# Attention, one-expert MoE and GLU on one core: scores made transposed in narrow array tiles, and fewer weight conversions in the last batch

## The chip, the cores and the metric

One core of one Trainium2 chip runs the whole kernel as one program. The metric is device time in microseconds (us), median over runs. The engines are named as the profile names them: PE (TensorE matmul), PEld (its weight loads), DVE (VectorE), ACT (ScalarE), POOL (GpSimd) and SP (SyncE, which issues nearly all DMAs here).

## The reference, cut to what matters

```python
B, H, S, Dh, M = 8, 8, 576, 64, 32
a   = softmax(phi, axis=2)                      # over the 576 positions
k_m = einsum('bhsm,bhsd->bhmd', a, k)           # 32 pooled keys of each head
v_m = einsum('bhsm,bhsd->bhmd', a, v)
attn = softmax(q @ k_m^T / 8, axis=-1)          # the scores: 576 x 32 of each head
x   = attn @ v_m                                # 4608 x 512
x   = moe(x)        # top-1 expert of 8, hidden 1024, relu, times its gate weight
out = (sigmoid(x @ w_gate) * (x @ w_val)) @ w_out    # GLU, width 1536
```

## The kernel before, in words

The program has two halves. The first takes the eight batches one after the other (the loop at L861). For a batch, `Expert` (L397) makes the hidden layer and the MoE output in two halves of 288 tokens. A half is eight units `hidden` (L402, six matmuls each) and eight units `y_part` (L416, twelve matmuls each), so a batch has 32 units, and their numbers 0 to 31 are called slots. Behind each unit the loop calls what `side(i)` (L540) has put into that slot for the batches to come: the softmax of phi, the pooling of keys and values, the scores of the next batch, its gating, and the fold of the pooled values into the expert's first weight (`fold`, L363). All of it shares the engines with the units. Tile's scheduler may move instructions from this order where no data forbids it.

The scores of one batch are made by `scores(t0)` (L253) for t0 = 0, 2 and 4, that is for 256, 256 and 64 tokens. A matmul has 128 (or 64) tokens of `qt` as its weights, and the 64 columns of `kmb` that hold the pooled keys of two heads are moved past them. The result lies with tokens on the partitions, 256 columns a token tile. DVE then takes the maximum of each head's 32 scores (L269) and subtracts it (L270). `normalize` (L272) has ACT's exponential, the sum and the reciprocal on DVE, and POOL's product. `attn_transpose` (L283) brings the result back by transposes into a bank of tag `tr`, from where ACT (`ahT`) and DVE (`alT`) take its high and low parts. The PSUM tags are `mm` (4 banks), `tr` (2), `sc` (1) and `kv` (1).

The same loop also converts the weights of the GLU from 64-bit floats, in 36 pieces (`Narrow`, L453): a DMA of 512 KB into a tile of tag `raw` (two buffers), one ACT operation (L468), five on DVE (L469 to L473), one on POOL (L474) and a DMA into `wd`. The table `NARROW` (L34) has for each batch the number of pieces, the pitch in slots and the slot of the first load. `pin` keeps a piece's instructions behind what stands ahead of them on their engines.

```python
NARROW = ((3, 6, 11), (4, 7, 0), (4, 7, 0), (4, 7, 0), (4, 7, 0), (4, 7, 0), (6, 4, 2), (7, 4, 0))
at(lead + pitch * k, pin, w.load)
at(lead + pitch * k + 5, pin, w.round)
at(lead + pitch * k + 7, pin, w.store)
```

In the last batch the loop also loads the first token block of the second half (`first_load`, L854), cuts it into sums and differences (`first_steps`, L857), and in slots 27 and 28 loads and prepares the weights of `quads[0]`. A quad's load (L737) takes a buffer of the same tag `raw`.

Between the halves stands `with tc.If(routed["rest"] > 0)` (L884). It runs the other seven experts where a token needs them; with this data it is skipped. Each engine meets this branch behind all of its work of the first half. Behind it `quads[1].load` (L930) comes first, and then the second half: for each of five token blocks 12 quads (L776) and the output product (L919 to L921).

## Time and profile before

| | us |
|---|---|
| median of three runs | 1317.14 (1316.63 to 1317.9) |
| the profiled execution | 1316.01 |
| its span in the trace | 1313.9 |
| PE busy | 1274.6 (97%) |
| DVE busy | 801.6 (61%) |
| ACT busy | 576.5 (44%) |
| POOL busy | 77.0 (6%) |

The span runs from the first to the last instruction of the program; the profiled execution's own time has some 2 us around it. A matmul's bar in the trace is its whole flight, longer than the step from one matmul to the next, so costs on PE are read from the starts of two instructions. Each fp32 matmul stands in the trace as two passes (a score matmul, a fold, a pooling); a matmul of the rounded parts and a transpose stand as one.

### The profile page before, as it was taken

The page shows a single profiled execution, that of the slowest core. Times are in us where ns is not written, and L with a number is a line of the kernel's source. Part 1 is how long each engine was busy: PE and PEld are TensorE (multiplying, and loading weights), DVE is VectorE, ACT ScalarE, POOL GpSimd, SP SyncE. Part 2 cuts the span into 40 slices and gives each one's busy share as a digit, 9 for nine tenths or more (in the row PEclk, how much of TensorE's full clock was granted, in tenths as well). Part 3 has the DMA queues.
Part 4 walks back from the last instruction along what each step waited for, and adds up shares of the span by engine and source line. Part 5 has one row for each costly group of instructions (what it writes and reads, how often), then busy time and mean ns, then how long its engine had stood idle before and what let it go on. Part 6 is the DMA issues. An engine that isn't in the chain of part 4 may idle for free.

```text
span 1313.9 us, 20107 instructions
## 1 busy us (share of the span) xinstructions
PE 1274.6 (97%) x7850; PEld 1136.5 (86%) x7850; DVE 801.6 (61%) x1593; ACT 576.5 (44%) x1125; POOL 77.0 (6%) x90
## 2 busy tenths in 40 slices
PE   7999999999999949999999999999999999999998
PEld 6899898998999949998899888998889988888787
DVE  4466566665659848786466754668446684466533
ACT  3343433333324316564365634556346563454422
POOL 3011011111112110000000000000000000000000
PEclk8899999999999979999999999999999999999999
DMA  8444543635325544342423424333243342423112
GB/s 346 170 152 148 186 150 119 213 109 185 103 88 169 151 138 144 128 153 80 153 97 128 137 82 151 126 118 134 73 144 128 129 137 80 160 97 116 45 41 88
DMA packets 68485, 173.93 MB, mean 132 GB/s; under 512 B 6944, under 2 KB 15648, under 8 KB 65312
## 3 DMA queue, kind: packets, MB, share of 16 engines
q1 hardware_dynamic: 67376, 171.47, 38.7%
q8 instruction: 63, 1.03, 0.3%
q10 hardware_dynamic: 1008, 1.11, 0.2%
q14 instruction: 38, 0.31, 0.1%
HBM read 137.95 MB, written 34.60 MB: 131 GB/s over the span
## 4 chain that ended last, share of the span: by engine, by line
PE 58%; DMA 2%; DVE 2%; ACT 0%; issue 0%; DVEq 0%; SPq 0%
PE pstr L776 21%; PE pskv L776 10%; PE pssc L776 5%; PE psmm L921 4%; PE psmm L919 4%; PE psmm L920 4%; PE pstr L919 1%; PE pstr L921 1%; PE pstr L920 1%; DMA xq<-x2d 1%; PE pssc L919 1%; PE pskv L919 1%; PE pssc L920 1%; PE pskv L921 1%; PE pssc L921 1%; PE pskv L920 1%
## 5 line engine op out<-in xcount | busy, mean ns | idle before, releaser
L776 PE MATMUL pstr<-xcvml,aw 128*128 128x448 f32 (+1 forms) x720 | 160.8, 371 | 3.9 <-DVE gw2h L788 3.8
L387 PE MATMUL psmm<-hh,w2h 128*128 128x288 f32 x512 | 157.2, 307 | 0.0
L388 PE MATMUL psmm<-hl,w2h 128*128 128x288 f32 x512 | 152.7, 298 | 0.2 <-DVE hl L414 0.2
L776 PEld LDWEIGHTS pstr<-xcvml,aw 128*128 128x128 f32 x720 | 133.4, 188 | 22.0 <-DVE gw2h L788 7.3
L389 PE MATMUL psmm<-hh,w2l 128*128 128x288 f32 x512 | 151.7, 296 | 0.0
L387 PEld LDWEIGHTS psmm<-hh,w2h 128*128 128x128 f32 x512 | 96.9, 189 | 13.6 <-issue 12.3
L117 DVE TENSOR_TENSOR aw<-raww,aw 128x512 fp32r<-128x512 f32 x120 | 66.0, 555 | 59.5 <-ACT aw L116 59.0
L776 PE MATMUL pstr<-xckv,aw 128*128 128x448 f32 (+1 forms) x360 | 86.0, 372 | 15.7 <-DVEq L884 13.9
L388 PEld LDWEIGHTS psmm<-hl,w2h 128*128 128x128 f32 x512 | 97.0, 189 | 0.7 <-DVE hl L414 0.4
L389 PEld LDWEIGHTS psmm<-hh,w2l 128*128 128x128 f32 x512 | 96.9, 189 | 0.0
L920 PE MATMUL psmm<-ow,gh 128*128 128x512 f32 x240 | 93.4, 389 | 0.0
L921 PE MATMUL psmm<-ow,gl 128*128 128x512 f32 x240 | 93.4, 389 | 0.0
L919 PE MATMUL psmm<-ow,gh 128*128 128x512 f32 x240 | 93.4, 389 | 0.0
L776 PEld LDWEIGHTS pstr<-xckv,aw 128*128 128x128 f32 x360 | 68.1, 190 | 23.1 <-issue 14.1
L776 PE MATMUL pstr<-xcvmh,aw 128*128 128x448 f32 (+1 forms) x360 | 84.4, 369 | 1.2 <-DVE tex L788 1.1
L776 PE MATMUL pssc<-xckv,aw 128*128 128x448 f32 (+1 forms) x360 | 84.3, 369 | 0.0
L776 PE MATMUL pskv<-xcvmh,aw 128*128 128x448 f32 (+1 forms) x360 | 84.0, 368 | 0.0
L776 PE MATMUL pskv<-xcxc,aw 128*128 128x448 f32 (+1 forms) x360 | 83.8, 368 | 0.0
L116 ACT CAST aw<-raww 128x512 fp32r<-128x512 f32 x120 | 60.4, 511 | 50.7 <-DMA raww<-wd 32.4
L387 PE MATMUL psmm<-ahT,vmh 128*128 128x288 f32 x256 | 80.2, 313 | 1.2 <-DVE vml L117 0.5
L388 PE MATMUL psmm<-alT,vmh 128*128 128x288 f32 x256 | 78.0, 305 | 0.3 <-DVE alT L117 0.3
L117 DVE TENSOR_TENSOR aw<-sums,aw 128x512 fp32r<-128x512 f32 x120 | 77.7, 685 | 0.3 <-ACT aw L116 0.3
(225 smaller groups left out, 2602.5 us busy)
## 6 DMA issues: line engine op xcount, KB each, us to landing
raww<-wd SPq DMA_DIRECT2D x60, 512.0 KB, 4.2
sums<-sd SPq DMA_DIRECT2D x48, 512.0 KB, 3.4
raw<-in_wgv_dram SPq DMA_DIRECT2D x36, 512.0 KB, 3.9
oraw<-wd SPq DMA_DIRECT2D x60, 256.0 KB, 2.6
kv<-in_kv_dram SPq DMA_DIRECT2D x9, 1024.0 KB, 9.1
qt<-in_q_dram SPq DMA_DIRECT2D x8, 1152.0 KB, 5.2
x2d<-yt SPq DMA_DIRECT2D x64, 144.0 KB, 2.5
wd<-f SPq DMA_DIRECT2D x36, 256.0 KB, 2.1
```

Of the source, the lines that this page charges most:

```text
L116: hi_copy(hi, src)
L117: lo_engine.tensor_tensor(out=lo, in0=src, in1=hi.bitcast(F32), op=ALU.subtract)
L387: T.matmul(pm, wh, xh, start=i == 0, stop=False)
L388: T.matmul(pm, wh, xl, start=False, stop=False)
L389: T.matmul(pm, wl, xh, start=False, stop=i == n - 1)
L776: T.matmul(o, wk, xk, start=start and k + a == 0, stop=k == KH - 1 and a == 2, skip_group_check=not start)
L919: T.matmul(o, gh, w[:, 0], start=c == 0, stop=False)
L920: T.matmul(o, gh, w[:, 1], start=False, stop=False)
L921: T.matmul(o, gl, w[:, 0], start=False, stop=c == NC2 - 1)
```

## The change

Scores are now made in two steps. `scores_in(t0)` has the pooled keys as weights, 64 rows by 32 columns, in eight positions of the array, and moves 256 (or 64) token columns of `qt` past them; the result, with heads and keys on the partitions, fills two banks (tag `tr` twice; `sc` and `kv` once in the prologue), and ACT copies both into a tile `st`. `scores(t0)` then brings `st` back by transposes into the bank that it filled before. What follows is unchanged. Two lines more of warm-up matmuls stand in the prologue. The table `NARROW` has five pieces in the second to the seventh batch and three in the last (the first keeps its three), and the load of `quads[0]` stands in slot 20. Lines from L253 on move down by 15, from `side` on by more.

```diff
--- before.py
+++ after.py
@@ -31,7 +31,7 @@
 TMAX = max(BLOCKS) // 2
 EPS = 1e-9
 NK = NC2 * F2 // D
-NARROW = ((3, 6, 11), (4, 7, 0), (4, 7, 0), (4, 7, 0), (4, 7, 0), (4, 7, 0), (6, 4, 2), (7, 4, 0))
+NARROW = ((3, 6, 11), (5, 6, 0), (5, 6, 0), (5, 6, 0), (5, 6, 0), (5, 6, 0), (5, 6, 0), (3, 5, 0))
 ORDER = mybir.DependencyInfo(mybir.DependencyClass.NoSync, mybir.DependencyReason.DATA)
 PARTS = (([0],), ([1],), ([0, 1], True))
 WARM = (9, 1, 6, 10)
@@ -155,6 +155,7 @@
             self.at_b = b if pair is None else 2 * pair + b
             self.first = b if pair is None else None
             self.ex = {}
+            self.st = {}
 
         def rows(self, t):
             if self.first is not None:
@@ -250,17 +251,31 @@
             src = pvw[:, : 2 * E].rearrange("p (g e) -> p g e", g=2)
             split(self.vw[:, :, :E], self.vw[:, :, E:], src)
 
+        def scores_in(self, t0):
+            n, rows = (2, P) if t0 < 4 else (1, 64)
+            km = kmb[self.odd]
+            w = n * P if n == 2 else rows
+            cols = slice(t0 * P, t0 * P + w)
+            st = ap.tile([P, 2, 2 * P], F32, name="st", bufs=2)
+            pst = [ps_one(tag) for tag in (("sc", "kv") if (self.first, t0) == (0, 2) else ("tr", "tr"))]
+            for c in range(4):
+                for g in range(2):
+                    r = slice(64 * ((c + g) % 2), 64 * ((c + g) % 2) + 64)
+                    T.matmul(pst[g][32 * c : 32 * c + 32, :w], km[r, 2 * g + c // 2, c % 2 * M : c % 2 * M + M], self.qt[r, 2 * g + c // 2, cols], start=True, stop=True)
+            for g in range(2):
+                A.copy(st[:, g, :w], pst[g][:, :w])
+            self.st[t0] = st
+
         def scores(self, t0):
             n, rows = (2, P) if t0 < 4 else (1, 64)
             if t0 == 0:
                 self.ahT = ap.tile([P, 2, S], F32R, name="ahT", bufs=2)
                 self.alT = ap.tile([P, 2, S], F32R, name="alT", bufs=2)
-            km = kmb[self.odd]
             psc = ps_one("mm" if self.first == 0 else "sc")
+            st = self.st.pop(t0)
             for i in range(n):
-                for p in range(NP):
-                    c = i * 256 + p * 64
-                    T.matmul(psc[:rows, c : c + 64], self.qt[:, p, (t0 + i) * P : (t0 + i) * P + rows], km[:, p, :], start=True, stop=True)
+                for g in range(2):
+                    T.transpose(psc[:rows, i * 256 + g * P : i * 256 + (g + 1) * P], st[:, g, i * P : i * P + rows], ident)
             g = n * H
             pv3 = psc[:rows, : n * 256].rearrange("p (g m) -> p g m", m=M)
             mx = ap.tile([P, 2 * H], F32, name="mx", bufs=2)[:rows, :g]
@@ -523,6 +538,7 @@
                     for a in two:
                         a.load_q()
                         for t in (0, 2, 4):
+                            a.scores_in(t)
                             a.scores(t)
                             a.normalize(t)
                             a.attn_transpose(t)
@@ -570,12 +586,15 @@
                 at(13, c.scale_kv)
                 at(14, c.keep_kv)
                 at(15, c.gate_cols)
+            at(6 + lag, c.scores_in, 0)
             at(7 + lag, c.scores, 0)
+            at(9 + lag, c.scores_in, 2)
             at(8 + lag, c.normalize, 0)
             at(10 + lag, c.scores, 2)
             at(10 + lag, c.normalize, 2)
             at(11 + lag, c.attn_transpose, 0)
             at(12 + lag, c.gate_logits, 0)
+            at(11 + lag, c.scores_in, 4)
             at(12 + lag, c.scores, 4)
             at(12 + lag, c.normalize, 4)
             at(13 + lag, c.attn_transpose, 2)
@@ -663,6 +682,9 @@
     w2_parts[2].low(V)
     w2_parts[3].split()
     warm(WARM[2])
+    b0.scores_in(0)
+    b0.scores_in(2)
+    warm(2)
     b0.scores(0)
     b0.scores(2)
     b0.normalize(0)
@@ -672,6 +694,8 @@
     warm(WARM[3], "kv")
     b0.attn_transpose(0)
     warm(WARM[3], "kv")
+    b0.scores_in(4)
+    warm(3, "kv")
     b0.scores(4)
     b0.attn_transpose(2)
     kept[1]()
@@ -868,7 +892,7 @@
                 (8, count_experts),
                 (24, late_x),
                 (25, first_steps, slice(8, None)),
-                (27, quads[0].load),
+                (20, quads[0].load),
                 (28, quads[0].prepare),
             ):
                 u.setdefault(slot, []).append(unit)
```

On PE, in one of the middle batches, the 64-token end of the scores stood before so (L303 and L305 are the gate's logits, L387 to L389 the unit's matmuls):

```order
L389 MATMUL psmm<-hh,w2l 128x288
L303 MATMUL pskv<-vw,ahT 128x16 x2
L305 MATMUL pskv<-vw,alT 128x8 x2
L303 MATMUL pskv<-vw,ahT 128x16 x2
L305 MATMUL pskv<-vw,alT 128x8 x2
L263 MATMUL pssc<-kmb_101,qt 64x64 x4
L387 MATMUL psmm<-hh,w2h 128x288
```

In the changed program PE has there (L305 now is `attn_transpose`, L264 `scores_in`, L402 to L404 the unit's matmuls):

```order
L404 MATMUL psmm<-hh,w2l 128x288
L305 MATMUL pstr<-ident,ex 128x128 x4
L264 MATMUL pstr<-qt,kmb_100 32x64 x4
L402 MATMUL psmm<-hh,w2h 128x288
L403 MATMUL psmm<-hl,w2h 128x288
L404 MATMUL psmm<-hh,w2l 128x288
L402 MATMUL psmm<-hh,w2h 128x288
L403 MATMUL psmm<-hl,w2h 128x288
L264 MATMUL pstr<-qt,kmb_100 32x64 x4
```

The end of the scores moved ahead, right behind `attn_transpose` of the first 256 tokens, and the scheduler split it: four matmuls into one `tr` bank, and four, five unit matmuls later, into the other, which is the bank that `attn_transpose` has just filled.

On DVE, the last rows ahead of the branch stood before so (L760 to L763 and L117 prepare `quads[0]`, L469 to L473 are a conversion, L426 is the y output):

```order
L426 TENSOR_TENSOR yt<-psmm,gb 128x288 x2
L760 TENSOR_TENSOR sums<-raww 128x256
L762 TENSOR_TENSOR sums<-raww 128x256
L117 TENSOR_TENSOR aw<-raww,aw 128x512
L761 TENSOR_TENSOR sums<-sums,raww 128x256
L117 TENSOR_TENSOR aw<-raww,aw 128x256
L763 TENSOR_TENSOR sums<-raww,sums 128x256
L469 TENSOR_SCALAR f<-f 128x512
L117 TENSOR_TENSOR aw<-sums,aw 128x512 x2
L470 TENSOR_SCALAR raw<-raw 128x512
```

Behind them came the conversion's last three operations and the branch. Now the rows there are (L441 is the y output, L429 the hidden layer's low part):

```order
L488 SCALAR_TENSOR_TENSOR raw<-raw 128x512
L429 SCALAR_TENSOR_TENSOR hl<-psmm,hh 128x288 x2
L117 TENSOR_TENSOR aw<-sums,aw 128x512
L429 SCALAR_TENSOR_TENSOR hl<-psmm,hh 128x288 x2
L117 TENSOR_TENSOR xcvmh_5775<-xq,xcvmh_5775 128x448
L429 SCALAR_TENSOR_TENSOR hl<-psmm,hh 128x288
L117 TENSOR_TENSOR xcvml_5776<-xq,xcvml_5776 128x448
L117 TENSOR_TENSOR xcvmh_5775<-xone,xcvmh_5775 128x448
L117 TENSOR_TENSOR xcvml_5776<-xtwo,xcvml_5776 128x448
L441 TENSOR_TENSOR yt<-psmm,gb 128x288 x4
L506 TENSOR_LOAD rest
L908 COMPARE_AND_BRANCH
```

The last conversion (L488 is its end) and the whole preparation now stand ahead of most of the second half's `hl`, and only the four y outputs are left ahead of the branch.

On SP, the end of the first half stood before so (L478 stores a conversion, L461 loads one, L395 stores y, L740 and L764 are the quad's load and the store of its sums):

```order
L461 DMA raw<-in_wgv_dram 128x1024
L395 DMA x2d<-yt 128x288
L478 DMA wd<-f 128x512
L740 DMA raww<-wd 128x2x512
L395 DMA x2d<-yt 128x288 x2
L764 DMA sd<-sums 128x1024
L478 DMA wd<-f 128x512
L884 COMPARE_AND_BRANCH
```

Now SP has (L493 stores a conversion, L410 stores y, L764 and L788 are the quad's):

```order
L410 DMA x2d<-yt 128x288
L493 DMA wd<-f 128x512
L764 DMA raww<-wd 128x2x512
L410 DMA x2d<-yt 128x288 x2
L788 DMA sd<-sums 128x1024
L410 DMA x2d<-yt 128x288
L493 DMA wd<-f 128x512
L410 DMA x2d<-yt 128x288 x4
L908 COMPARE_AND_BRANCH
```

Four stores of y, those of the batch's second half, now stand between the last conversion's store and the branch, where there was none.

## Rows read from the trace of the kernel before

**Rows 1.** The page's second part: granted clock in 40 slices.
```profile
PEclk8899999999999979999999999999999999999999
```

**Rows 2.** Stretches (length; busy PE, PEld, DVE, ACT, POOL; clock): middle, last batch, join.
```profile
165.90:223.20 57.30, 56.27 (x498) 51.96 (x497) 34.66 (x92) 19.04 (x47) 7.92 (x7) 0.97 0.45 149
...
277.40:331.40 54.00, 53.97 (x498) 50.38 (x497) 33.61 (x87) 18.06 (x44) 7.95 (x7) 1.00 0.46 156
...
430.50:470.00 39.50, 38.77 (x290) 38.08 (x288) 30.73 (x64) 11.71 (x26) 7.84 (x6) 1.00 0.51 158
470.00:492.70 22.70, 6.10 (x21) 4.93 (x21) 8.83 (x20) 4.67 (x10) 1.28 (x1) 0.70 0.38 122
```

**Rows 3.** Timeline of PE over the join (start, length, what, idle before).
```profile
469.68 0.29 PE L389 MATMUL psmm<-hh,w2l 128*128 128x288 f32 x1
483.89 2.58 PE L776 MATMUL pstr<-xckv,aw 128*128 128x448 f32 x6 [13.92 <-DVEq L884]
...
492.68 0.67 PE L776 MATMUL pstr<-xcvml,aw 128*128 128x448 f32 x2 [0.96 <-DVE gw2h L788]
```

**Rows 4.** Timeline of SP's DMA issues over the join.
```profile
470.43 0.89 SPq L395 DMA_DIRECT2D x2d<-yt  x2
...
482.09 0.33 SPq L478 DMA_DIRECT2D wd<-f  x1
486.26 0.92 SPq L740 DMA_DIRECT2D raww<-wd  x2
```

**Rows 5.** The branch by itself: line 884's instructions on the sequencers (length, start).
```profile
L884 DVEq EVENT_SEMAPHORE  x2: 21/21/21, 483.7 to 483.8; - x2
...
L884 DVEq COMPARE_BRANCH  x1: 72/72/72, 480.6 to 480.6; - x1
...
L884 SPq COMPARE_BRANCH  x1: 50/50/50, 482.5 to 482.5; - x1
```

**Rows 6.** Timeline of DVE over the join.
```profile
470.01 0.46 DVE L426 TENSOR_TENSOR yt<-psmm,gb 128x288 f32<-128x288 f32 x1 [2.59 <-PE psmm L389]
...
479.96 0.69 DVE L473 SCALAR_TENSOR_TENSOR raw<-raw 128x512 f32<-128x512 uint16 x1
```

**Rows 7.** Timeline of PE around a 256-token score group, and at the 64-token end.
```profile
165.91 0.29 PE L389 MATMUL psmm<-ahT,vml 128*128 128x288 f32 x1
166.04 1.89 PE L263 MATMUL pssc<-kmb,qt 128*128 128x64 f32 x16
...
167.96 0.29 PE L388 MATMUL psmm<-hl,w2h 128*128 128x288 f32 x1
...
178.87 0.68 PE L263 MATMUL pssc<-kmb,qt 128*64 128x64 f32 x8
179.47 0.40 PE L387 MATMUL psmm<-hh,w2h 128*128 128x288 f32 x1
```

**Rows 8.** Timeline of PE around one fold (L373, 16 passes) and one pooling (L227, 40).
```profile
371.78 0.29 PE L389 MATMUL psmm<-hh,w2l 128*128 128x288 f32 x1
...
373.26 0.30 PE L388 MATMUL psmm<-hl,w2h 128*128 128x288 f32 x1
...
301.14 0.29 PE L387 MATMUL psmm<-ahT,vmh 128*128 128x288 f32 x1
...
302.84 0.29 PE L389 MATMUL psmm<-ahT,vml 128*128 128x288 f32 x1
```

**Rows 9.** Timeline of PE around the four transposes of `attn_transpose(0)`.
```profile
175.83 0.29 PE L389 MATMUL psmm<-hh,w2l 128*128 128x288 f32 x1
...
176.53 0.29 PE L388 MATMUL psmm<-hl,w2h 128*128 128x288 f32 x1
```

**Rows 10.** Timeline of DVE in the same place.
```profile
177.23 0.68 DVE L117 TENSOR_TENSOR alT<-pstr,ahT 128x512 fp32r<-128x512 f32 x1
```

**Rows 11.** Groups by line, middle batches: ACT from PSUM, DVE's longest conversion operation.
```profile
L413 ACT ACTIVATE hh<-psmm 128x288 fp32r<-128x288 f32 x89 | 36.6, 411 | 31.1 <-PE psmm L389 30.1 <-PE pstr L216 0.8
...
L471 DVE SCALAR_TENSOR_TENSOR f<-f,raw 128x512 int32<-128x512 int32 x26 | 18.5, 712 | 0.2
```

## The prediction

> **What bounds the kernel now.** I read the stretches first. In a calm middle batch PE works 53.97 of 54.00 us, and DVE and ACT 33.61 and 18.06 [rows 2]: PE's own instructions set the time there. The batch before it shows what a disturbed one costs: 57.30 us, of which PE worked 56.27, and a granted clock of 0.97, which is a short piece at 1.2 instead of 2.4 GHz. The one long hole is the join between the halves: in 22.70 us PE worked 6.10 [rows 2].
>
> The timelines then tell what the hole waits for. PE's last matmul of the first half starts at 469.68 and ends at 469.97; the next starts at 483.89, released by DVE's branch, and PE runs on without holes from 492.68 [rows 3]. DVE had made its last y by 470.47, but was kept by the preparation of `quads[0]` and by the last conversion, whose last operation ends at 480.65 [rows 6]. Its branch is taken at 480.6, and its first semaphore behind it comes at 483.7 [rows 5]: 3.1 us for the branch itself. SP is later still. It stores the last conversion at 482.09, takes the branch at 482.5 and issues the load of `quads[1]` at 486.26 [rows 4, 5]. The load, its landing and its preparation lead to PE at 492.68, 6.4 us later. So the hole is made by conversions in the last batch that run over its end.
>
> **The join.** The change leaves three conversions in the last batch instead of seven and loads `quads[0]` in slot 20 instead of 27. In the order of the changed program the last conversion and the whole preparation stand on DVE ahead of most of the second half's `hl`, and on SP the last conversion's store stands ahead of four stores of y. What remains behind PE's last matmul is one y on DVE (to 470.47 [rows 6]) and the two y stores on SP, which before were issued at 470.43 and took 0.89 [rows 4]. SP would take the branch at 471.4 instead of 482.5, **11.1 us earlier**, and everything from `quads[1]` on moves with it: its load to 475.2, PE's unbroken work to 481.6. DVE's branch moves to 470.5 and PE's first product to about 473.8, so the first quad's products still lie ahead of the second quad's. Bounds: no gain at all (the load comes late anyway), and 16.6 us, the whole idle time of PE in that stretch, 22.70 less 6.10 [rows 2]. I take 11.1, since both ends of SP's chain are read from rows.
>
> **The scores on PE.** PE's normal step from matmul to matmul is 0.13 us, as from 165.91 to 166.04 [rows 7]; I measure a group from the matmul ahead of it to the second behind it and take off two steps. A 256-token group cost 167.96 - 165.91 - 0.26 = 1.79 us, and the 64-token end 179.47 - 178.87 = 0.60 [rows 7]. A batch: 2 x 1.79 + 0.60 = 4.18 us.
>
> The new matmuls have the fold's form: 64 x 32 weights in eight places. A fold costs 1.48 - 0.26 = 1.22 us for two rounds of 512 columns, that is 1024; a pooling, four places of 128 x 32, costs 1.70 - 0.26 = 1.44 us for ten rounds of 128, that is 1280 [rows 8]. The line through both is 0.34 us for going into the narrow form and out of it, and 0.86 ns a column. Two rounds of 256 columns then cost 0.34 + 0.44 = 0.78, and the end, split in two by the scheduler, twice 0.34 and 0.11 between them, some 0.8. Four transposes cost 0.70 - 0.26 = 0.44 [rows 9], twice in a batch, and the two of the end between 0.22 and 0.44, taken as 0.3. A batch now: 2 x 0.78 + 0.8 + 2 x 0.44 + 0.3 = 3.54 us, a saving of **0.64 us**.
>
> Against it stands a new wait. The second half of the end goes into the `tr` bank that `attn_transpose(0)` has filled, and must wait until DVE's `alT` has left it. Before, the transposes started one step after 175.83, at 175.96, and `alT` ended at 177.23 + 0.68 = 177.91 [rows 9, 10]. PE would have done the transposes at 176.3, the first half (0.4) at 176.7 and the five matmuls at 177.4, and would stand some 0.5 us. All unit matmuls behind stand with it. Net 0.64 - 0.5 = 0.1 us a batch, in seven batches **0.7 us gained**. Ends: without the wait 4.5 us gained; with one more DVE operation of 0.71 [rows 11] ahead of `alT`, 4.3 us lost.
>
> **The copies.** Six more ACT operations a batch, at most 0.41 us each (the nearest row is a PSUM read of 288 columns [rows 11], the new ones have 256 and 64), 2.5 us on an engine that works 18.06 of 54 [rows 2]. They are hidden by the unit matmuls that the order puts between `scores_in` and its transposes: six in the first group, 0.8 us, and twelve in the second. Two copies end some 0.8 us after the group, so the first transposes just about come off. Cost taken: 0; if that cover fails, 0.8 us a batch. The Trainium skill (TensorEngine Tiling (Array Packing), Performance Considerations, PSUM Bottleneck) warns that narrow tiles speed up the matmuls but not the emptying of PSUM, so the copies can become the limit. No row of this kernel shows that yet; it is the second rival below.
>
> **Conversions moved.** Batches 2 to 6 (counted from 1) get one more each, five in all; the seventh loses one, the last four. On DVE a conversion is five operations of at most 0.71 [rows 11], so at most 3.6 us more on an engine with 20 us idle in the calm batch [rows 2]. Hidden, unless it lands in front of something PE waits for. I take **0.5 us lost** in all, between 0 and the 3.3 us a batch by which the disturbed batch is longer than the calm one [rows 2]. In the last batch PE idled 0.73 of 39.5 us with DVE busy 30.73 [rows 2]; that can come back, or the preparation, now ahead of the second half's `hl` and `hh`, can hold them for 1.5. I take 0.
>
> **The prologue** has the first batch's scores on its path: ten transposes, 24 narrow matmuls and five warm-up matmuls for 20 score matmuls. PE's work stays about even, since the warm-ups' ten passes are 1.1 us at 0.11 a pass (1.79 over 16 [rows 7]); but copies of up to 0.41 now lie between the steps. I take **0.5 us lost**, between 0 and 2. The lower clock of the first two slices, and of the fifteenth, which holds the join [rows 1], I leave out of the sum.
>
> **Sum:** -11.1 - 0.7 + 0.5 + 0.5 = **-10.8 us**. The profiled execution took 1316.01, so it would take 1305.2. The median of the runs shown is 1317.14, 1.1 above that execution, and with the same difference the forecast is **1306.3**.
>
> **Rivals.**
>
> *The wait moves into the last batch* (0.08). The preparation needs the load of `quads[0]`, the load a `raw` buffer, the buffer the end of the second conversion. ACT's `aw` now stands ahead of the second half's `hh`. If the load lands late, `hh` waits, and after four `mm` banks PE too. For it speaks the tight chain; against it that three conversions need far less time than the batch's 39.5 us [rows 2]. A load and preparation that are exposed cost the 6.4 us from SP's issue to PE at the join [rows 3, 4], less the 3.2 us of four banks (six matmuls of 0.13 each): 3.2 lost, 1309.5.
>
> *The copies bind* (0.06). By the rule of the Trainium skill named above this is what narrow tiles would bring. As a mechanism here: PE reaches the transposes before ACT has copied. With the first group's two copies bare, 0.8 us in seven batches, 1312; with all six bare, 2.5 us, and a gain of 11.1 undone by 17.5, less the wait counted above: about 1320. Against it speak ACT's 36 idle microseconds a batch.
>
> *The clock falls in the batches* (0.05), the case on the slower side. The split end gives each batch an idle piece that it had not; the disturbed batch, with 1.03 us of idle pieces, also lost clock (0.97 [rows 2]). If six more batches become like that one, at 3.3 us each, the time is 1306.3 + 19.8 = 1326. It decides for slower from 1.9 us a batch on. Against it: the last batch had 0.73 us of idle pieces and kept its clock at 1.00 [rows 2].
>
> *The join does not open* (0.03): PE is held there by something that the profile puts down to DVE only because DVE came last. Then 1306.3 + 11.1 = 1317.4. Against it speaks that SP's own chain is as long.
>
> **How the numbers follow.** About 0.2%, 2.6 us, is what a measurement of this kernel can tell from no change: faster means below 1314.5, slower above 1319.8. The forecast's own case has 0.78, at 1301 to 1311 by the ends of the waits at the split end, the prologue and the conversions. The first rival lies in the same range. The range of eight in ten is 1300 to 1312.5. Faster: 0.78 + 0.08 + 0.04 of the copies' case = 0.90; same 0.04; slower 0.06.
>
> **What would show it.** Right: PE's hole between its last `w2h` matmul and the second half's first product (L800 in the changed program) about 4 us long instead of 13.9, SP's branch 1.5 us behind PE's end, the load of `quads[1]` 5 us behind it; a narrow group of 16 passes at about 0.8 us; an idle gap of about 0.5 us in the middle of the split end, released by `alT`; middle batches of 54 us as before. Wrong: gaps ahead of the transposes released by the `st` copies; a clock below 1.00 in several middle batches; a hole in the last batch ahead of `hh`; or batches shorter by 0.6, which would mean that the second half never waits.

## The result, and the profile after

The changed kernel takes **1301.33 us** (median of four runs, 1296.45 to 1302.29) beside 1317.03 of the kernel before (four runs, 1316.63 to 1317.9): a ratio of **0.9874** over the runs (that of the two medians is 0.9881), 95% interval 0.9858 to 0.9891, faster by 15.7 us. The forecast was 1306.3, range 1300 to 1312.5. So the sign, the range and the largest term held, and the size was short by 5 us. The sections below show that several terms were short by more than that in sum, and that a loss which had been put at nothing hid a part of it.

The profiled execution, which the rows come from, is the fastest of the four, 1296.45, and some 5 us below the other three. Sums of its rows (19.3 us less than the span of before) are therefore larger than the difference of the medians, and are compared with the prediction's terms one by one.

The join, by the timeline of PE (it answers to [rows 3]):

```profile
463.83 0.29 PE L404 MATMUL psmm<-hh,w2l 128*128 128x288 f32 x1
468.00 1.50 PE L800 MATMUL pstr<-xckv,aw 128*128 128x448 f32 x6 [3.88 <-DVEq L908]
```

and by SP's DMA issues (they answer to [rows 4]):

```profile
464.65 0.33 SPq L410 DMA_DIRECT2D x2d<-yt  x1
468.65 0.38 SPq L764 DMA_DIRECT2D raww<-wd  x1
```

The branch by itself, line 908's instructions on the sequencers (they answer to [rows 5]):

```profile
L908 DVEq EVENT_SEMAPHORE  x2: 21/21/21, 467.8 to 467.9; - x2
...
L908 DVEq COMPARE_BRANCH  x1: 72/72/72, 464.8 to 464.8; - x1
L908 SPq COMPARE_BRANCH  x1: 50/50/50, 465.0 to 465.0; - x1
```

PE's hole is 3.88 us instead of 13.92. DVE takes the branch at 464.8, 0.2 us behind its last `yt`, and signals at 467.8; SP takes it at 465.0, right behind the last store of y, and issues the load of `quads[1]` at 468.65, only 0.65 behind PE's first product (before, 2.4 behind it). PE has no hole in the 14 us after that, where before it had two, 1.74 and 0.96. It works at half clock for 3.4 us behind its first product (469.2 to 472.6), about as long as before (483.89 to 487.2). Most of what is left of the join is the branch itself: 3.0 of 4.17 us lie between DVE's branch and its signal.

The stretches show where the rest of the span went. Each row is a stretch with its length, the busy time of PE, PEld, DVE, ACT and POOL, and the granted clock: batches 4, 6, 7 and 8 (counted from 1, each from its first hidden-layer matmul), the join, and the second half. They answer to [rows 2].

```profile
210.35:263.40 53.05, 53.05 (x516) 47.98 (x514) 37.48 (x97) 20.84 (x53) 9.25 (x9) 1.00 0.51 176
...
317.03:370.64 53.61, 53.12 (x515) 47.97 (x514) 36.91 (x92) 20.08 (x50) 9.26 (x9) 1.00 0.36 119
370.64:421.54 50.90, 48.64 (x416) 44.21 (x414) 43.92 (x103) 20.98 (x48) 10.16 (x9) 1.00 0.40 129
421.54:463.83 42.29, 39.82 (x291) 39.38 (x290) 25.29 (x56) 12.06 (x27) 5.06 (x4) 0.96 0.37 116
463.83:468.00 4.17, 0.29 (x3) 0.09 (x2) 0.46 (x1) 0.00 (x0) 0.00 (x0) 1.00 0.13 43
468.00:1294.58 826.58, 818.84 (x3816) 715.08 (x3816) 494.59 (x808) 405.89 (x729) 0.00 (x0) 1.00 0.35 115
```

The middle batches are 53.05 us long and PE works in all of it: still PE's own instructions, one microsecond fewer. Batches 5 and 6 have half a microsecond of idle time each, the seventh 2.26. The last batch is longer than before (42.29 beside 39.19), and this is why. The timeline of PE there:

```profile
443.14 0.29 PE L404 MATMUL psmm<-ahT,vml 128*128 128x288 f32 x1
445.90 0.61 PE L402 MATMUL psmm<-ahT,vmh 128*128 128x288 f32 x1 [2.47 <-DVE yt L441]
```

that of ACT:

```profile
442.40 0.93 ACT L116 CAST aw<-raww 128x512 fp32r<-128x512 f32 x2 [3.41 <-DMA raww<-wd]
444.13 1.29 ACT L116 CAST aw<-sums 128x512 fp32r<-128x512 f32 x2 [0.81 <-DVE sums L785]
445.33 1.00 ACT L428 ACTIVATE hh<-psmm 128x288 fp32r<-128x288 f32 x3
```

that of DVE (L784 is the preparation's first operation, L441 the y output):

```profile
442.40 0.42 DVE L784 TENSOR_TENSOR sums<-raww 128x256 f32<-128x256 f32 x1 [3.17 <-DMA raww<-wd]
...
445.39 0.45 DVE L441 TENSOR_TENSOR yt<-psmm,gb 128x288 f32<-128x288 f32 x1
```

and of SP's issues:

```profile
437.13 0.38 SPq L764 DMA_DIRECT2D raww<-wd  x1
```

The load of `quads[0]` is issued at 437.13 and lands at 442.40, and two engines wait for it. ACT's four `aw` casts are ahead of the second half's `hh`, so the first `hh` comes at 445.33. On DVE seven operations of the preparation are ahead of the first half's last `yt`, which runs from 445.39 to 445.84. PE has made three units of the second half by 443.14, one `mm` bank each; the fourth bank still holds what that `yt` reads. So PE stands 2.47 us, and what releases it is DVE's `yt`, not ACT's `hh`. Behind that hole the clock falls to half for 3.4 us, as this stretch shows (columns as above):

```profile
445.40:448.80 3.40, 2.90 (x12) 2.90 (x13) 3.40 (x10) 1.34 (x5) 0.00 (x0) 0.50 0.51 198
```

Last, the narrow scores. The timeline of PE at the first 256-token group of a batch (it answers to [rows 7]; L264 are the 16 passes of `scores_in`, L278 the transposes):

```profile
162.71 0.29 PE L404 MATMUL psmm<-ahT,vml 128*128 128x288 f32 x1
162.92 0.66 PE L264 MATMUL pstr<-qt,kmb 64*32 64x256 f32 x16
...
163.75 0.30 PE L403 MATMUL psmm<-alT,vmh 128*128 128x288 f32 x1
...
164.28 0.30 PE L404 MATMUL psmm<-ahT,vml 128*128 128x288 f32 x1
164.42 0.60 PE L278 MATMUL pssc<-ident,st 128*128 128x128 f32 x4
...
164.99 0.30 PE L403 MATMUL psmm<-hl,w2h 128*128 128x288 f32 x1
```

and the copies on ACT:

```profile
163.68 0.65 ACT L266 COPY st<-pstr 128x256 f32<-128x256 f32 x2 [0.16 <-PE pstr L264]
```

By the prediction's measure the group costs 163.75 - 162.71 - 0.26 = 0.78 us and its transposes 164.99 - 164.28 - 0.26 = 0.45. The two copies end at 164.33 and the first transpose starts at 164.42: covered, with 0.09 us to spare. The second half of the 64-token end on PE:

```profile
173.85 0.29 PE L403 MATMUL psmm<-hl,w2h 128*128 128x288 f32 x1
174.08 0.32 PE L264 MATMUL pstr<-qt,kmb 64*32 64x64 f32 x8
```

and the `alT` of the first 256 tokens on DVE:

```profile
173.77 0.68 DVE L117 TENSOR_TENSOR alT<-pstr,ahT 128x512 fp32r<-128x512 f32 x1
```

The second half of the end starts 0.23 us behind the last unit matmul, at 174.08, as a narrow group does without a wait (162.92 behind 162.71 above), while `alT` runs until 174.45. It does not wait for `alT`, which reads the bank that `attn_transpose` filled, so it goes into another bank than that one.

### The profile page after: what moved, and what is told of

Its sections match the earlier page's. It is cut to its first block, busy times and chain, and to the rows that moved or that the text cites. A ratio compares the mean times of both kernels' runs of the same rounds, so it can differ in the third digit from the quotient of the medians.

```text
span 1294.6 us, 20500 instructions
## 1 busy us (share of the span) xinstructions
PE 1263.6 (98%) x8004; PEld 1115.4 (86%) x8004; DVE 807.2 (62%) x1593; ACT 586.7 (45%) x1173; POOL 78.3 (6%) x90
## 3 DMA queue, kind: packets, MB, share of 16 engines
q8 instruction: 65, 1.06, 0.3%
## 4 chain that ended last, share of the span: by engine, by line
PE 58%; DMA 3%; DVE 2%; ACT 0%; issue 0%; DVEq 0%; SPq 0%
PE pstr L800 21%; PE pskv L800 10%; PE pssc L800 5%; PE psmm L945 4%; PE psmm L944 4%; PE psmm L943 4%; DMA xq<-x2d 2%; PE pstr L944 1%; PE pstr L945 1%; PE pstr L943 1%; PE pssc L944 1%; PE pssc L945 1%; PE pskv L945 1%; PE pskv L944 1%; PE pssc L943 1%; PE pskv L943 1%
## 5 line engine op out<-in xcount | busy, mean ns | idle before, releaser
L402 PE MATMUL psmm<-hh,w2h 128*128 128x288 f32 x512 | 157.6, 308 | 0.0
L404 PE MATMUL psmm<-hh,w2l 128*128 128x288 f32 x512 | 151.8, 297 | 0.0
L402 PEld LDWEIGHTS psmm<-hh,w2h 128*128 128x128 f32 x512 | 96.4, 188 | 15.6 <-issue 14.8
L117 DVE TENSOR_TENSOR aw<-raww,aw 128x512 fp32r<-128x512 f32 x120 | 66.0, 555 | 58.9 <-ACT aw L116 58.2
L404 PEld LDWEIGHTS psmm<-hh,w2l 128*128 128x128 f32 x512 | 96.2, 188 | 0.8 <-issue 0.2
L402 PE MATMUL psmm<-ahT,vmh 128*128 128x288 f32 x256 | 81.6, 319 | 2.8 <-DVE yt L441 2.5
L117 DVE TENSOR_TENSOR aw<-sums,aw 128x512 fp32r<-128x512 f32 x120 | 78.2, 689 | 0.0
L404 PE MATMUL psmm<-ahT,vml 128*128 128x288 f32 x256 | 76.7, 300 | 0.0
```

What stands on the lines that cost most here:

```text
L117: lo_engine.tensor_tensor(out=lo, in0=src, in1=hi.bitcast(F32), op=ALU.subtract)
L402: T.matmul(pm, wh, xh, start=i == 0, stop=False)
L404: T.matmul(pm, wl, xh, start=False, stop=i == n - 1)
```

## The experiments

Nine more kernels and the changed one again ran, in three groups; each group has its own runs of the kernel before on the same chip (medians 1315.11, 1313.42 and 1315.28), so ratios to that kernel are what is compared across groups. **Lengths of stretches** come from one profiled execution each.

### The two parts of the change apart

One kernel has the new scores with the old table and `quads[0].load` in slot 27, the other the old scores with the new table and slot 20. (The slot is no third part: with slot 27 in the changed kernel the order of the instructions on all five engines is row for row what it is with slot 20, so that was not run.) The edit shown is the first kernel's, of the changed one; the second kernel is the one before with the same lines the other way round.

```diff
-NARROW = ((3, 6, 11), (5, 6, 0), (5, 6, 0), (5, 6, 0), (5, 6, 0), (5, 6, 0), (5, 6, 0), (3, 5, 0))
+NARROW = ((3, 6, 11), (4, 7, 0), (4, 7, 0), (4, 7, 0), (4, 7, 0), (4, 7, 0), (6, 4, 2), (7, 4, 0))
-                (20, quads[0].load),
+                (27, quads[0].load),
```

> The scores in narrow tiles alone; the table of conversions and the slot of quads[0].load as before. Theory (parts add; the narrow scores are worth about 0.95 us a batch on PE, and the two batches that lost clock in the trace of before lose it no more): 1307 to 1311, PE's hole at the join 13 to 14 us as before, middle batches 53.0 to 53.3 us long, and the batch's scores about 0.77 us cheaper than before. Rival 1 (the prediction's 0.1 us a batch, the rest came from the conversions): 1315.5 to 1317, batches of 54 us. Rival 2 (the shorter batches came from the evenly spread conversions, not from the scores): batches of 54 to 57 us and 1316 to 1318.

> The table of conversions and the slot of quads[0].load as changed; the scores as before. Theory: the join opens (PE's hole some 4 us instead of 13.9, and 3 us less behind it), the last batch has the new hole of some 2.5 us ahead of hh and a piece at half clock: 1305 to 1309, middle batches 54 us. Rival 1 (conversions alone bring all): 1300 to 1303. Rival 2 (five conversions in a batch disturb the gating of the old order): middle batches of 55 to 57 us and 1310 to 1316.

> The changed kernel once more, for the scatter of its runs and as the bar for what runs beside it. Theory (1301.3 is the usual time, and the profiled execution at 1296.45 met a better stretch of clock): median 1300.5 to 1302.5 in the timed runs. Rival (a profiled execution is itself shorter): the profiled one again some 5 us below the timed ones.

Scores alone: 1311.81, ratio 0.9971 (0.9957 to 0.9986). Table alone: 1305.85, ratio 0.9929 (0.9911 to 0.9948). Both, the changed kernel again: 1297.52 (1295.8 to 1300.08), ratio 0.9872 (0.9855 to 0.9889). The ratio of the changed kernel is that of the first comparison; its time is not, nor is that of the kernel before, so the absolute numbers of all three expectations were tied to runs that were slower by 2 to 4 us. The table alone came out as its theory had it, the scores alone just above the range of theirs (1307 to 1311): batches 5 and 7 got longer, which that theory did not have. It also speaks of two batches that lost clock before; batch 2 was long at a granted clock of 1.00, only batch 3 had lost some (0.97). Neither case of the third one holds: the profiled execution is again the fastest, but 1.7 us below the median and 1.0 below the next, which is the scatter of these runs. The 5 us of the first comparison stay unexplained.

Lengths in us (the last row from PE's first second-half product to the end):

| | before | scores alone | table alone | both |
|---|---|---|---|---|
| batch 1 | 69.91 | 68.95 | 70.08 | 68.94 |
| batch 2 | 55.16 | 53.80 | 54.12 | 53.16 |
| batch 3 | 57.29 | 53.32 | 54.01 | 53.04 |
| batch 4 | 54.19 | 53.76 | 54.02 | 53.05 |
| batch 5 | 54.01 | 55.18 | 54.59 | 53.63 |
| batch 6 | 53.90 | 53.30 | 54.58 | 53.61 |
| batch 7 | 51.38 | 54.06 | 54.80 | 50.90 |
| batch 8 | 39.19 | 39.17 | 43.96 | 42.29 |
| join | 14.21 | 14.36 | 4.17 | 4.17 |
| second half | 829.98 | 830.22 | 827.86 | 826.58 |

Three things follow. The join belongs to the table: with the scores alone PE stands as long as before, by its timeline:

```profile
481.10 0.71 PE L800 MATMUL pstr<-xckv,aw 128*128 128x448 f32 x1 [14.07 <-DVEq L908]
```

The calm batch belongs to the scores: under the new table, batches 2 to 6 shrink by 0.96 or 0.97 each. (Under the old one, with its disturbed batches, the change is anything from 3.97 less to 1.17 more.) And the hole in the last batch belongs to the table too; it stands in the kernel with the old scores, with the same preparation ahead of `yt` and `hh` and the clock at 0.96 over the batch. Table alone, the stretch of the last batch:

```profile
430.87:474.83 43.96, 40.74 (x291) 39.74 (x290) 25.54 (x57) 12.06 (x27) 5.76 (x4) 0.96 0.34 112
```

its timeline of PE:

```profile
456.67 0.42 PE L387 MATMUL psmm<-ahT,vmh 128*128 128x288 f32 x1 [2.65 <-DVE yt L426]
```

and of ACT:

```profile
453.17 0.93 ACT L116 CAST aw<-raww 128x512 fp32r<-128x512 f32 x2 [2.53 <-DMA raww<-wd]
```

The parts do not add up in these traces: 2.6 and 7.0 us of span apart, 19.3 together. Most of the surplus sits in batches 7 and 8, which the scores alone lengthen by 2.7, the table alone by 8.2 and both together by 2.6. In the seventh, old scores under the new table stand 1.63 us for `ahT` and 1.46 for the gating, and lose clock (0.97); new scores under the old table stand 1.84 us for POOL's `ex` and lose more. Scores alone, the stretch of the seventh batch:

```profile
373.51:427.57 54.06, 51.75 (x418) 47.22 (x417) 43.74 (x109) 21.69 (x49) 12.93 (x9) 0.94 0.44 137
```

and the wait in PE's timeline:

```profile
400.70 0.47 PE L305 MATMUL pstr<-ident,ex 64*128 64x64 f32 x2 [1.84 <-POOL ex L296]
```

By the ratios the surplus is 16.8 - 3.8 - 9.3 = 3.7 us, and the three intervals, each some 2 us to either side, leave open whether it is there at all.

### The preparation held back

```diff
-                (28, quads[0].prepare),
+                (28, pin, quads[0].prepare),
```

> The changed kernel with the preparation of quads[0] held behind slot 28 on its engines, so that ACT's aw casts stand behind the second half's hh instead of ahead of them. Theory (the hole of 2.47 us in the last batch and the 3.4 us at half clock behind it come from aw waiting for the load): hole gone, last batch 39 to 40 us instead of 43.1, 1296.5 to 1299 beside 1301.3, the join's hole up by at most 1. Rival (the preparation costs at the join what it cost in the last batch): join hole 6 to 8 us and 1300 to 1303.

Measured: 1297.62, ratio 0.9874 (0.9856 to 0.9892). The stretches of the last batch and the join:

```profile
424.63:463.96 39.33, 38.62 (x292) 38.15 (x290) 24.52 (x56) 12.30 (x27) 5.44 (x4) 1.00 0.39 125
463.96:468.14 4.18, 0.29 (x3) 0.08 (x2) 0.46 (x1) 0.00 (x0) 0.00 (x0) 0.78 0.13 45
```

and the longest hole of PE in that batch:

```profile
448.04 0.40 PE L402 MATMUL psmm<-ahT,vmh 128*128 128x288 f32 x1 [0.70 <-DVE hl L429]
```

The cause is as the theory had it: with the preparation behind the second half's units the batch is 39.33 us, the hole 0.70, and nothing of it comes back at the join. The load is issued as late as ever, at 440.03, 15.4 us into the batch (15.6 in the changed kernel). `pin` holds the preparation back on ACT and on DVE at once, so this run does not part the two. The median does not show it. Beside it the changed kernel's own last batch was 40.90 with a hole of 1.88 and no fall of the clock behind it, so 1.6 us were to be had, and this execution lost as much in its first batch (71.72 us beside 70.00, with a second stretch at half clock from 80.6 to 87.4, behind a hole of 1.24; all kernels with the new scores have a hole of 1.24 to 1.39 there, and only here was it followed by such a stretch).

### What narrow groups cost, and what covers the copies

The first kernel drops the third group and gives the second one 320 columns. The second keeps it, but in the banks `tr` and `sc`, and the order no longer splits it. The third takes the six unit matmuls between the first group and its transposes away, in six batches; `pin` keeps the instructions in that order, and `run1` just calls.

```diff
-            w = n * P if n == 2 else rows
+            w = 2 * P if t0 == 0 else S - 2 * P
...
-            at(11 + lag, c.scores_in, 4)
```
```diff
-            pst = [ps_one(tag) for tag in (("sc", "kv") if (self.first, t0) == (0, 2) else ("tr", "tr"))]
+            pst = [ps_one(tag) for tag in (("sc", "kv") if (self.first, t0) == (0, 2) else ("tr", "sc") if t0 == 4 else ("tr", "tr"))]
```
```diff
-            at(6 + lag, c.scores_in, 0)
+            at(7 + lag, c.scores_in, 0)
...
-            at(9 + lag, c.scores_in, 2)
+            at(9 + lag, *((pin, c.scores_in, 2) if i else (c.scores_in, 2)))
...
         for unit in ex.units():
-            run([unit])
+            if 0 < i < B - 1 and s == 8:
+                pin(unit[0], *unit[1:])
+            else:
+                run([unit])
...
-                    T.transpose(psc[:rows, i * 256 + g * P : i * 256 + (g + 1) * P], st[:, g, i * P : i * P + rows], ident)
+                    (pin if t0 == 0 and (self.first or 0) > 1 else run1)(T.transpose, psc[:rows, i * 256 + g * P : i * 256 + (g + 1) * P], st[:, g, i * P : i * P + rows], ident)
```

> The changed kernel with the end of the scores joined to the second group: two groups a batch, of 256 and of 320 columns, and no third one. Theory (going into the narrow form and out of it costs 0.34 us whatever the columns, and a column 0.86 ns): the two halves of the end, 0.45 and 0.44 us in the trace, become 0.11 us in the second group, which takes 0.90 instead of 0.79; 0.77 us a batch, calm batches of 52.3 us instead of 53.05, and 0.9945 to 0.9975 of the changed kernel, some 1291 to 1294 beside 1297.5. Rival (the columns cost, not the entries): the second group 0.99 us or more and a gain of under 2 us in all.

Measured: 1290.34, ratio 0.9832 (0.981 to 0.9855); a calm batch of 52.27 us. Seven times 0.78 is 5.5; the ratio is 0.0040 under that of the changed kernel, 5.3 us. The second group in PE's timeline:

```profile
218.11 0.29 PE L405 MATMUL psmm<-hh,w2l 128*128 128x288 f32 x1
218.33 0.77 PE L263 MATMUL pstr<-qt,kmb 64*32 64x320 f32 x16
219.03 0.40 PE L403 MATMUL psmm<-hh,w2h 128*128 128x288 f32 x1
219.27 0.30 PE L404 MATMUL psmm<-hl,w2h 128*128 128x288 f32 x1
```

It costs 219.27 - 218.11 - 0.26 = 0.90, as worked out: 64 columns more in each of two rounds cost 0.11, and a third group, split in two by the order, had cost 0.89. So the entry is what a short group pays for: here the 0.22 us from 218.11 to 218.33 and the 0.24 from 219.03 to 219.27 stand where a unit's step is 0.13, and these two steps make 0.20 of the 0.34 us. The Trainium skill (TensorEngine Tiling (Array Packing), Tiling Modes, Key Properties) says that a change of the tiling mode drains the engine. These longer steps agree with it.

> The changed kernel with the 64-token end in two different banks (tr and sc instead of tr twice), so that the order no longer splits it. Theory: one entry into the narrow form less, the end 0.45 us in place of 0.45 and 0.44, batches of 52.6 us instead of 53.05, 2 to 3 us less in all, 1294.5 to 1296 beside 1297.5. Rival (the sc bank is still read by the subtraction of the second group, and the end waits for DVE): a gap of 0.3 us or more ahead of the end, released by DVE, and 1297 to 1300.

Measured: 1298.21, ratio 0.9874 (0.9853 to 0.9895), a calm batch of 53.04 instead of the 52.6 expected: nothing gained. The end itself costs 0.47 us as it should, 0.41 less than in two halves. But PE then comes too early to the gate's logits of the next tokens (timeline of PE):

```profile
235.02 0.37 PE L318 MATMUL pskv<-vw,ahT 128*128 128x16 f32 x2
235.62 0.39 PE L320 MATMUL pskv<-vw,alT 128*128 128x8 f32 x2 [0.23 <-DVE alT L117]
235.87 0.37 PE L318 MATMUL pskv<-vw,ahT 128*128 128x16 f32 x2
```

with, on DVE:

```profile
234.89 0.67 DVE L117 TENSOR_TENSOR alT<-pstr,ahT 128x512 fp32r<-128x512 f32 x1
```

From 235.02 to 235.62 are 0.60 us where the same two matmuls behind it take 0.22 (235.87 to 236.09): 0.38 given back, in a wait that the row shows as 0.23. Neither theory had this place: the rival's wait is there, released by DVE, but not for the `sc` bank.

> The changed kernel with the unit matmuls between the first group and its transposes taken away in six batches: the transposes stand right behind the group, so that the two copies on ACT lie bare. Theory (the copies bring no cost because the order puts six unit matmuls over them; bare they cost the 0.81 us from the group's end to the second copy's end): a gap of 0.6 to 0.8 us ahead of these transposes, released by ACT's st, batches of 53.6 to 53.9 us, 4 to 5 us more in all, 1301 to 1303 beside 1297.5. Rival (PE is not what sets the batch's time once the scores are narrow, another engine is): batches of 53.05 us as they are, and no difference.

Measured: 1301.91, ratio 0.9903 (0.9883 to 0.9923), calm batches of 53.74, 0.70 more than 53.05; in six batches 4.2 us, and the ratios differ by 0.0031, 4.1 us. The wait in PE's timeline:

```profile
219.48 0.71 PE L465 MATMUL pssc<-ident,st 128*128 128x128 f32 x3 [0.52 <-ACT st L266]
```

and the copies in ACT's:

```profile
219.05 0.65 ACT L266 COPY st<-pstr 128x256 f32<-128x256 f32 x2 [0.23 <-PE pstr L264]
```

So the copies are free by the order alone. This is the mechanism of the second rival, and its price was near (0.8 a batch was set). The rule of the Trainium skill that the prediction named (TensorEngine Tiling (Array Packing), Performance Considerations, PSUM Bottleneck) is that the copies may become the limit. They do in this trace, where nothing covers them, and not in that of the changed kernel, where PE works 53.05 of 53.05 us.

### Versions that beat both

The joined end, the preparation held back, and the last two batches with four conversions each, off the seventh batch's gating; then the same, and the changed kernel itself, without the two added lines of warm-up matmuls.

```diff
-NARROW = (... (5, 6, 0), (3, 5, 0))
+NARROW = (... (4, 7, 2), (4, 5, 0))
```
```diff
-    warm(2)
...
-    warm(3, "kv")
```

> The end joined to the second group, the preparation held behind slot 28, and the seventh batch with four conversions from slot 2 in steps of 7 and the last with four in steps of 5. Theory: 5 us from the joined end, 2 from the last batch, and up to 2 from the seventh batch, where the conversion that met the gating (holes of 0.80 and 1.46 us) is moved off it: 1288 to 1292 beside 1297.5, a last batch of 39.3 us. Rival (the fourth conversion makes the last batch late again, or the holes of the seventh come from something else): no better than the joined end alone, a join of more than 5 us or holes of 2 us in the seventh batch.

Measured: 1285.56 (1283.53 to 1286.78), ratio **0.9788** (0.9768 to 0.9808). The stretches of batches 7 and 8:

```profile
365.73:414.11 48.38, 47.79 (x399) 43.82 (x398) 41.11 (x99) 20.30 (x45) 10.60 (x8) 1.00 0.39 127
414.11:452.40 38.29, 38.29 (x291) 38.09 (x290) 27.19 (x60) 12.66 (x28) 6.31 (x5) 1.00 0.42 140
```

The last batch has no idle time at all with four conversions in it, and the seventh 0.59 instead of 2.26. The time lies below the range expected (1288 to 1292, set beside 1297.5 from a group whose kernel before was 1.7 slower), and the last batch a microsecond below its 39.3. Against the joined end alone that is 50.07 to 48.38 and 42.84 to 38.29: 6.2 us, and the ratios differ by 5.8.

> The changed kernel without its two added lines of warm-up matmuls in the prologue (two and three matmuls, ten passes). Theory (the first line lies in the time that ACT needs for the copies, the second costs six passes, 0.8 us, on PE's path): the idle piece ahead of the first transposes 1.2 to 1.6 us instead of 0.82 to 0.98, the first batch starting 0 to 0.8 us earlier than at 35.2 to 35.5, and no difference that the median shows beside the changed kernel's 0.9872. Rival (without them the clock falls longer in the first batch): another 3.4 us piece at half clock ahead of 100 us, and 1.7 to 3.4 us more.

> The joined end, the held preparation and the last two batches with four conversions each, now without the two added lines of warm-up matmuls. Theory: as with them, 0.977 to 0.980 of the kernel before, first batch earlier by up to 0.8 us. Rival (the clock needs them): 1.7 to 3.4 us more, 0.981 to 0.982.

Measured: 1297.49, ratio 0.9866 (0.9844 to 0.9889), for the changed kernel without the two lines, and 1285.85, ratio 0.9775 (0.975 to 0.9799), for the best version without them: no difference from 0.9872 and 0.9788 that these runs can tell. PE reaches the first batch's first matmul at 34.98 (35.2 and 35.4 with them) and at 34.16 (35.28), and half clock lasts 10.2 and 6.8 us in that batch, as it does with them (6.8 and 10.2 in the changed kernel's two profiles). PE's wait ahead of the first transposes is 1.08 us instead of 0.82 and 0.98, a little under what was expected. In the changed kernel without the lines the end's transposes, whose copies the second line had covered, wait too (timeline of PE):

```profile
33.45 0.41 PE L278 MATMUL psmm<-ident,st 128*64 128x128 f32 x2 [0.41 <-ACT st L266]
```

## Why the prediction was right, and where its steps were not

| step | predicted | shown by the rows |
|---|---|---|
| join and what lies behind it | -11.1 | -10.0 and -3.4 |
| scores on PE, a batch | -0.64, and +0.5 waited | -0.77, nothing waited, -0.2 elsewhere |
| copies | 0 | 0; 0.70 a batch if bare |
| conversions moved | +0.5 | +2.3 waited in batches 5 to 7, -4.3 in 2 and 3 |
| last batch | 0 | +3.1 |
| prologue | +0.5 | +0.6 to the first unit |

**The join** was right in its cause and its times: SP's branch 1.2 us behind PE's last start (1.7 forecast), the load of `quads[1]` 4.8 behind it (5.5), PE's first product 4.2 (4.1). The step "PE's unbroken work to 481.6" was too late: it carried the 6.4 us from SP's load to PE along, though with the load only 0.65 us behind PE's first product the products of `quads[0]` cover it. The two holes that are gone with it, 1.74 and 0.96, are 2.7 of the 3.4 us behind the join; the rest is not accounted for. The table alone has the join and 2.1 of the 3.4, with half clock for 5.2 us behind its first product.

**The scores** were mis-sized by one step, "must wait until DVE's `alT` has left it". The saving on PE's own instructions is 0.77 us: two groups as forecast (0.78 and 0.79), their transposes as forecast (0.45 each), an end of 0.45 and 0.44 (two rounds in each half, where the 0.8 of the forecast had one), and for its two transposes some 0.07 instead of 0.3 (logits and transposes together 1.06, where logits and score matmuls had been 1.59 and the score matmuls 0.60 of that). The two long groups gain 0.56 each, and the end loses 0.35. But the second half never waited (174.08, above). The prediction, and the section on the change, took the second half to go into the bank that `attn_transpose` had filled. In the built program the second half's first matmul waits for ACT alone: it goes into the bank that ACT's copy of the first half has emptied. The text had named this outcome: batches shorter by 0.6 "would mean that the second half never waits". The other 0.2 us of a calm batch's 0.97 come from a place that the prediction never looked at: under the old scores PE stood at the gate's logits for `alT`. With the table alone two of these matmuls take 0.41 us from start to start (timeline of PE):

```profile
236.71 0.37 PE L303 MATMUL pskv<-vw,ahT 128*128 128x16 f32 x2
237.12 0.38 PE L305 MATMUL pskv<-vw,alT 128*128 128x8 f32 x2
```

and in the changed kernel 0.22:

```profile
233.42 0.37 PE L318 MATMUL pskv<-vw,ahT 128*128 128x16 f32 x2
233.64 0.36 PE L320 MATMUL pskv<-vw,alT 128*128 128x8 f32 x2
```

The unsplit end shows how near this is to being the limit: 0.41 us more were gained on PE, and this same wait took 0.38 back.

**Conversions moved** left out a gain. The step counted what five more conversions could hold up, and that happened: batches 5 and 6 wait 0.52 and 0.49 and the seventh 2.26 instead of 0.97. It left out that the old table, four conversions in steps of seven slots, had a part in what disturbed batches 2 and 3: with the new table and the old scores they are 54.12 and 54.01 instead of 55.16 and 57.29. With the new scores and the old table they are calm as well (53.80 and 53.32), so it took both old parts to disturb them. What the term comes to hangs on the scores beside it: from the old table to the new one, batches 2 to 7 together get 0.2 us longer under the old scores (325.9 to 326.1, since the seventh loses 3.4) and 6.0 shorter under the new ones (323.4 to 317.4). The prediction had the row of the 57.30 us batch in hand [rows 2] and used it as a price only.

**The last batch**, taken as 0, lost 3.1 us. This is the first rival, put at a chance of 0.08: its place, its late load, and a preparation that stands ahead of what empties the `mm` banks. The engine was another one first: the rival had ACT's `aw` ahead of `hh` and four full banks, and the rows have PE stopped after three units by DVE's `yt`. Its price of 3.2 is near by luck. It was the 6.4 us of a load at the join less the work in four banks; what was lost is a hole of 2.47 us and 3.4 us at half clock, and in the changed kernel's second profile, where the clock did not fall, 1.7 (40.90 beside 39.19). The argument against it, that three conversions need far less time than the batch, missed the point: the preparation stood too early for its load. ACT reached the casts at 439.0 and waited 3.41 us for a load that had been issued at 437.13. Held back behind slot 28 it costs nothing, with the load no earlier.

So the sum came out short by a wait that was not there, by the wait at the logits and the holes behind the join that went away, and by a gain in batches 2 and 3, and was brought closer again by the loss in the last batch. The join's 10 us are the mechanism that was forecast; that the rest left the time inside the range is in part luck. Two of the signs that the prediction named for being wrong were there: the hole in the last batch, and batches shorter by more than 0.6.

One sum among its rivals does not fit: with six batches like the disturbed one, slower begins at (1319.8 - 1306.3) / 6 = 2.25 us a batch; the 1.9 that it states goes with seven.

## What to carry to other kernels

Price a narrow tile group as an entry plus its columns. Here that is 0.34 us and 0.86 ns a column, set by two rows of the kernel before; two rounds of 64, 256 and 320 columns then come to 0.45, 0.78 and 0.89 and took 0.45, 0.78 to 0.79 and 0.90. The same 64 tokens cost 0.89 us as two groups of their own and 0.11 as 64 columns more of the group ahead. Before counting a saving on the bound engine, look for the next wait that it will run into; a wait that already stands by a few tenths in the trace takes the saving back. And a preparation moved early is only safe if the engines that run it have nothing urgent queued behind it: its place in their order decides, not the slot of its load.

## What the runs showed of the hardware that was not expected

From PE's last start to its next the join took 4.16 to 4.18 us in nine of the ten profiles with the new table, whatever stood ahead of it (4.28 in the tenth). In the changed kernel 3.0 us of it lie between DVE's branch at 464.8 and its first signal at 467.8. No run here tried to take the branch away.

The clock fell behind most holes of the last batch, but not by their place alone: behind 2.47 us (half clock from 445.4 to 448.8), behind 2.65 with the table alone, behind 2.44 with the joined end, but not behind 1.88 in the changed kernel's second profile nor behind 0.70 with the preparation held back. No run here varied the hole alone, so no rule is drawn from it. With the same program the stretches at half clock differ from execution to execution (one in the first batch from 39.2 to 46.0, then from 38.8 to 49.0), while the calm batches agree to 0.01. This is one source of the scatter of 2 to 5 us between runs, and not the only one. Two runs of the first comparison with the same mean granted clock, 0.993, took 1296.45 and 1301.29. And PE's waits for DVE's `gw2h` in the second half add up to 1.8 us in the profile of the best version and to 4.7 in that of the same without the two lines, whose second halves are 825.04 and 828.85 us long.
